# Decode attention with feed-forward on one core: q projection with column groups and held weights, q spread by one matmul per batch row and two quads, TensorE loop from unit 1

## Chip, core, metric

One core of one Trainium2 chip. The metric is the device time of one launch in microseconds (us). Most runs of the kernel before lie between 993.6 and 994.7 us; 4 of its 36 runs in this study are over 995 us.

## The reference

```python
# B=4 rows, one token each; D=640; 32 heads of 192; 4096 cached keys and values per head; F=1536
h   = x + attention(layernorm(x))       # q = ln(x) @ wq ; softmax(q k^T / sqrt(192)) v ; @ wo
out = h + (silu(ln(h) @ w_gate) * (ln(h) @ w_up)) @ w_down
```

The two caches are 403 of the 424 MB that the kernel reads. Every cached byte is used once.

## The kernel before

The work is cut in 32 *units*: a unit is four heads (one *quad*) of one batch row. For each unit one key load and one value load of 6.29 MB come in, all issued by SyncE on one DMA queue, in program order. I call them K0, K1, ... and V0, V1, ... by unit. There are two key buffers and one value buffer.

```python
def load_k(u):   # two slots: K(u) may start when the products of unit u-2 are done
    deps = [lambda: tk["tt", u - 2, NQ - 1]] if u >= 2 else ([wq_used] if u == 1 else [])
def load_v(u):   # one slot: V(u) may start when the values matmuls of unit u-1 are done
    deps = [(lambda: tk["pv", u - 1]) if u >= 1 else wq_used]

load_k(0); load_k(1)
for u in range(NU - 1):
    load_v(u)
    if u + 2 < NU:
        load_k(u + 2)
```

So the queue gets K0, K1, V0, K2, V1, K3, V2, ... and V1 is issued only after the values matmuls of unit 0, which run inside unit 1. One unit, shortened:

```python
for k in range(4):           # four quarters of the keys
    tt(u, k)                 # VectorE: keys * q, 128x6144, waits K(u) and q of this unit (qbc[u // 2])
    if k == 3: pv(u - 1)     # TensorE: values matmuls of the unit before -> frees the value slot
    red(u, k)                # TensorE: 12 identity matmuls fold 192 products to 16 (waits all of q)
    rsum(u, k - 1)           # VectorE
# then max, exp (ScalarE), and so on
```

The start, before unit 0: q projection (80 matmuls of 384 columns, four column groups), four copies of q, and the *spread*: each row's q is copied to the 32 partitions of its head by 128 small matmuls and 16 ScalarE evictions. The TensorE program is a hardware loop over units 2 to 31 (`pr.roll("pe", 2, NU)`); units 0 and 1 stand unrolled before it.

## Time and profile before

| | |
|---|---|
| time | 994.0 us (993.87 to 994.07), profiled span 992.2 us |
| busy | TensorE 58%, VectorE 56%, ScalarE 11% |
| DMA | 428 GB/s over the span; nine tenths or more in 39 of 40 slices |
| steady part | one key and one value load per 29.07 us, 433 GB/s |

From the page of the kernel before: busy time with share and number of instructions, the DMA row of the 40 slices (tenths busy), and the first two lines of the chain of work that ended last.

```profile
PE 577.5 (58%) x4656; PEld 117.2 (12%) x3248; DVE 552.7 (56%) x451; ACT 108.0 (11%) x348; POOL 3.4 (0%) x19
...
DMA  9999999999999999999999999999999999999997
...
DMA 67%; PE 18%; DVE 13%; SPq 1%; issue 0%; ACT 0%; DVEq 0%
DMA k<-in_A_k_cache_dram 60%; PE pb L152 11%; DVE prod L403 11%; DMA v<-in_A_v_cache_dram 8%; PE pb L455 5%; PE pb L411 2%; DVE sc L416 1%; SPq L350 0%; PE pb L551 0%; SPq L354 0%; PE pb L561 0%; PE pb L495 0%; DVE guT L557 0%; PE pb L480 0%; PE pb L298 0%
```

The kernel is bound by the DMA engines. The timeline of SyncE's queue in the kernel before (start us, duration, line, what is issued):

```profile
30.27 0.33 SPq L342 DMA_DIRECT2D k<-in_A_k_cache_dram  x1
30.64 0.43 SPq L350 DMA_DIRECT2D v<-in_A_v_cache_dram  x1
53.98 0.33 SPq L342 DMA_DIRECT2D k<-in_A_k_cache_dram  x1
76.36 0.33 SPq L350 DMA_DIRECT2D v<-in_A_v_cache_dram  x1
76.74 0.43 SPq L342 DMA_DIRECT2D k<-in_A_k_cache_dram  x1
101.11 0.33 SPq L350 DMA_DIRECT2D v<-in_A_v_cache_dram  x1
```

These are K1, V0, K2, V1, K3, V2. When V1 is issued at 76.36 us, only K2 is still moving. The first product starts when K0 has landed (VectorE, same timeline):

```profile
37.47 6.63 DVE L403 TENSOR_TENSOR prod<-k,qball 128x6144 f16<-128x6144 bf16 x2 [12.55 <-DMA k<-in_A_k_cache_dram]
```

And the windows view around V1's issue (window, length, then busy us and instructions of PE, PEld, DVE, ACT, POOL, the granted TensorE clock as a share of the full one, the DMA engines' share and GB/s; this view counts a packet whole in the window in which it starts, so a share can be over 1):

```profile
76.00:78.00 2.00, 2.00 (x17) 0.10 (x1) 0.42 (x1) 0.42 (x1) 0.00 (x0) 1.00 0.91 393
78.00:80.00 2.00, 1.83 (x19) 1.02 (x14) 0.91 (x2) 0.00 (x0) 0.00 (x0) 1.00 0.86 369
80.00:82.00 2.00, 0.76 (x4) 0.38 (x4) 1.49 (x5) 0.62 (x3) 0.00 (x0) 1.00 0.91 393
```

### The profile page before, as it was taken

Reading aid. Unit: us, or ns where it says so; the run is one execution under the profiler, and the core shown is the slowest. Engines: PE = TensorE matmul, PEld = TensorE weight load, DVE = VectorE, ACT = ScalarE, POOL = GpSimd, SP = SyncE. Lnnn points to the kernel's source line nnn. Section 1 sums busy time; section 2 is a strip of 40 time slices with the busy share of each in tenths; the row PEclk is TensorE's granted clock in tenths of the full one; section 3 lists DMA queues with packets and bytes.
Section 4 is the critical chain, followed back from the end, with each engine's and each line's share of the span. In section 5 each row is a group of like instructions: output and inputs, shape, how many; then the busy total and the mean of one; then the engine's idle time right before and its main releaser. Section 6 shows DMA issues by size and latency. Waiting matters only on the chain.

```text
span 992.2 us, 9305 instructions
## 1 busy us (share of the span) xinstructions
PE 577.5 (58%) x4656; PEld 117.2 (12%) x3248; DVE 552.7 (56%) x451; ACT 108.0 (11%) x348; POOL 3.4 (0%) x19
## 2 busy tenths in 40 slices
PE   0766555676555566655557655555665555666545
PEld 0101111111001111001111100111110011110032
DVE  1486645566654556664555666455666545566602
ACT  0311111110011110001111000111100111110011
POOL 1000000000000000000000000000000000000000
PEclk9788778887777888777788877788887778887775
DMA  9999999999999999999999999999999999999997
GB/s 402 427 436 433 423 438 438 420 442 436 420 444 434 422 444 430 426 440 430 430 440 428 432 440 424 432 442 422 436 440 422 438 438 422 440 436 420 421 417 306
DMA packets 12671, 424.48 MB, mean 428 GB/s; under 512 B 1264, under 2 KB 1264, under 8 KB 3952
## 3 DMA queue, kind: packets, MB, share of 16 engines
q1 hardware_dynamic: 12608, 424.29, 99.3%
q8 instruction: 7, 0.11, 0.0%
q14 instruction: 8, 0.07, 0.0%
q10 hardware_dynamic: 48, 0.01, 0.0%
HBM read 424.29 MB, written 0.01 MB: 428 GB/s over the span
## 4 chain that ended last, share of the span: by engine, by line
DMA 67%; PE 18%; DVE 13%; SPq 1%; issue 0%; ACT 0%; DVEq 0%
DMA k<-in_A_k_cache_dram 60%; PE pb L152 11%; DVE prod L403 11%; DMA v<-in_A_v_cache_dram 8%; PE pb L455 5%; PE pb L411 2%; DVE sc L416 1%; SPq L350 0%; PE pb L551 0%; SPq L354 0%; PE pb L561 0%; PE pb L495 0%; DVE guT L557 0%; PE pb L480 0%; PE pb L298 0%
## 5 line engine op out<-in xcount | busy, mean ns | idle before, releaser
L403 DVE TENSOR_TENSOR prod<-k,qball 128x6144 f16<-128x6144 bf16 x128 | 426.3, 3351 | 200.8 <-DMA k<-in_A_k_cache_dram 200.8
L152 PE MATMUL pb<-prod,identH 128*128 128x512 f16 x1408 | 385.8, 431 | 0.0
L411 PE MATMUL pb<-prod,identH 128*128 128x512 f16 x128 | 57.9, 452 | 340.5 <-DVE prod L403 334.2
L416 DVE TENSOR_REDUCE sc<-pb 128x32 f32<-128x512 f32 x128 | 88.0, 688 | 114.0 <-PE pb L152 114.0
L455 PE MATMUL pb<-v,pbuf 128*8 128x384 bf16 x2048 | 90.8, 330 | 9.2 <-DMA v<-in_A_v_cache_dram 9.1
L461 ACT ACTIVATE otmp<-pb,mask 128x192 f32<-128x192 f32 x32 | 13.4, 420 | 678.2 <-PE pb L455 678.2
L411 PEld LDWEIGHTS pb<-prod,identH 128*128 128x128 f16 x128 | 13.2, 103 | 588.0 <-DVE prod L403 466.7
L444 ACT ACTIVATE pbuf<-sc,negM 32x128 bf16<-32x128 f32 x128 | 73.4, 574 | 2.7 <-ACT negM L438 0.2
L455 PEld LDWEIGHTS pb<-v,pbuf 128*8 128x8 bf16 x2048 | 46.8, 87 | 121.3 <-DMA v<-in_A_v_cache_dram 86.6
L465 DVE SCALAR_TENSOR_TENSOR orow<-pb,mask,otmp 128x192 f32<-128x192 f32 x32 | 13.4, 418 | 77.4 <-ACT otmp L461 77.4
L444 ACT ACTIVATION_READ_ACCUMULATOR pbuf<-sc,negM 32x1 f32 x128 | 31.7, 248 | 0.0
L480 PE MATMUL pb<-pick,orow 128*64 128x2 f32 x384 | 22.3, 231 | 2.9 <-DVE orow L465 1.0
L438 ACT ACTIVATE negM<-pb 128x4 f32<-128x4 f32 x32 | 5.5, 173 | 161.1 <-PE pb L434 161.1
L470 PEld LDWEIGHTS pb<-lsb,halfm 128*128 128x128 f32 x64 | 12.1, 190 | 72.1 <-issue 71.1
L480 PEld LDWEIGHTS pb<-pick,orow 128*64 128x64 f32 x384 | 19.6, 174 | 6.2 <-DVE orow L465 1.7
L434 PE MATMUL pb<-negMc,ones_row 1*128 1x4 f32 x64 | 12.2, 258 | 11.9 <-DVE negMc L429 11.9
L429 DVE TENSOR_REDUCE negMc<-pb 1x4 f32<-1x128 f32 x32 | 8.9, 279 | 15.1 <-PE pb L425 15.1
L425 PE MATMUL pb<-identF,msb 128*1 128x128 f32 x64 | 12.2, 271 | 8.3 <-DVE msb L421 8.2
L298 PE MATMUL pb<-mv,quadm 128*128 128x2 f32 x4 | 1.2, 364 | 23.5 <-DVE mv L296 23.5
L434 PEld LDWEIGHTS pb<-negMc,ones_row 1*128 1x128 f32 x64 | 9.4, 183 | 21.3 <-DVE negMc L429 21.3
L294 DVE BATCH_NORM_STATS2 stats<-xrow 128x6 f32<-128x160 bf16 x1 | 0.3, 327 | 17.6 <-DMA xrow<-in_A_x_dram 17.6
L495 PE MATMUL pb<-wo_a,OTall 128*4 128x160 bf16 x144 | 5.2, 335 | 7.9 <-DMA wo_a<-in_A_wo_dram 6.7
(66 smaller groups left out, 92.0 us busy)
## 6 DMA issues: line engine op xcount, KB each, us to landing
k<-in_A_k_cache_dram SPq DMA_DIRECT2D x32, 6144.0 KB, 39.9
v<-in_A_v_cache_dram SPq DMA_DIRECT2D x31, 6144.0 KB, 25.7
wq_sb<-in_A_wq_dram SPq DMA_DIRECT2D x1, 7680.0 KB, 21.2
wo_a<-in_A_wo_dram SPq DMA_DIRECT2D x1, 5760.0 KB, 39.5
v<-in_A_v_cache_dram SPq DMA_DIRECT2D x1, 3072.0 KB, 20.6
wo_b<-in_A_wo_dram SPq DMA_DIRECT2D x1, 1920.0 KB, 13.7
wg_sb<-in_B_w_gate_dram SPq DMA_DIRECT2D x1, 1920.0 KB, 28.7
wu_sb<-in_B_w_up_dram SPq DMA_DIRECT2D x1, 1920.0 KB, 32.1
```

The costliest lines, as they stand in the source:

```text
L152: return e.add_instruction(mybir.InstMatmult(name=e.bass.get_next_instruction_name(), engine=mybir.EngineType.PE, start_tensor_calc=start, ...
L403: op("dve", lambda e: e.tensor_tensor(out=prod[BUF[k]][:, :, :], in0=kslot[u % 2][:, k * QT:(k + 1) * QT, :], in1=qball[:, u, None, :].bro ...
L411: op("pe", lambda e, j=j: (e.matmul if j == 0 else partial(held_matmul, e))(psR[k][:, 0:QT * R], lhsT=identH[:, :], rhs=prod[BUF[k]][:, :, ...
L416: op("dve", lambda e: e.tensor_reduce(sc[u % 2][:, k * QT:(k + 1) * QT], psR[k][:, 0:QT * R].rearrange("q (t r) -> q t r", r=R), AX.X, ALU ...
L425: op("pe", lambda e: e.matmul(psS[0:1, XT], lhsT=msb[:, 0:1], rhs=identF[:, :], start=True, stop=True), [g("rmax", u), g("negM", u - 1), p ...
L434: op("pe", lambda e: e.matmul(psS[:, XB], lhsT=ones_row[0:1, :], rhs=negMc[0:1, :], start=True, stop=True), [g("hmax", u), g("negM", u - 1 ...
L444: op("act", lambda e, h=h, r=r: e.activation(out=pbuf[r, :, h], in_=sc[u % 2][r, :], func=ACTF.Exp, bias=negM[r, h:h + 1], scale=alpha, ac ...
L455: op("pe", lambda e, t=t, n=n: e.matmul(psO[32 * n:32 * n + 8, 0:2 * DH], lhsT=pbuf[:, t:t + 2, :].rearrange("q t m -> q (t m)"), rhs=vslo ...
L461: op("act", lambda e: e.activation(out=otmp[:, :], in_=psO[:, 0:DH], func=ACTF.Copy, scale=mask[:, 0:1]), [g("pv", u), g("stt", u - 1), km ...
L465: op("dve", lambda e: e.scalar_tensor_tensor(out=orow[:, :], in0=psO[:, DH:2 * DH], scalar=mask[:, 1:2], in1=otmp[:, :], op0=ALU.mult, op1 ...
L470: op("pe", lambda e: e.matmul(psL[:, XL], lhsT=halfm[:, :], rhs=lsb[:, :], start=True, stop=True), [g("exp", u), g("otm", u - 1)], key=("l ...
L480: op("pe", lambda e, j=j, s=s, lo=lo: e.matmul(psL[64 * s:64 * s + 64, lo:lo + 2], lhsT=orow[:, j:DH:3], rhs=pick[:, s:4:2], start=True, s ...
```

## The change

Its intent is a shorter start and a smaller TensorE program: a head of the quad becomes a column group of the q projection, so that one weight load serves four matmuls; one 128x128 matmul spreads a row's q for two quads at once (16 matmuls for 128); and the loop starts one unit earlier.

```diff
+        for c in range(CD):                      # contraction chunk outermost
+            for k in range(4):
+                for n in range(4):
+                    rhs = ...                    # head n of two quads
+                    mm = partial(held_matmul, size=(128, 32), position=(0, 32 * n)) if k and HELD else ...
+                    a = op("pe", ... mm(e, PB[k][32 * n:32 * n + B, 0:2 * DH], lhsT=lnT[:, c, 0:B], rhs=rhs, ...))
+                if c == CD - 1:                  # the four copies now come together, at the end
+                    qcopy.append(op("act", ... qsb[:, k, :] <- PB[k] ...))
 ...
+        for i in range(NU // 2):
+            k, b, bank = i // B, i % B, psQ[i % 2]
+            a = op("pe", ... e.matmul(bank[:, 0:2 * DH], lhsT=sel[:, b, :], rhs=qsb[:, k, :], ...))
+            qbc[i] = op("act", ... qball[:, 8 * k + b:8 * k + b + B + 1:B, :] <- bank, scale=QS ...)
 ...
     def tt(u, k):
-            [landed["k", u], qbc[u // 2], last], key=("tt", u, k))
+            [landed["k", u], qbc[NU // 2 - 1 if FASTQ else u // 2], last], key=("tt", u, k))
 ...
-        pr.roll("pe", 2, NU)
+    pr.roll("pe", 1 if FASTQ else 2, NU)
```

Cut: the new layout of `OTall` (unit outermost), the larger `sel`, the code that computes loop waits, and two switches that stay off (`LOOPS`; `LATE`, which would load the last values before the last part of wo). A product now waits for the last of the 16 evictions of q, not for the one of its unit.

More of the change, by code (lines that the diff above doesn't have):

```diff
@@ L12 @@
 FP16 = mybir.dt.float16
-ROLL = True
+LOOPS = False
+FASTQ = True
+LATE = False
+HELD = True
 class Cfg:
@@ L46, in __init__ @@
         self.rolled = {}
+        self.shift = 0
     def op(self, eng, fn, deps=(), key=None):
@@ L112, in body @@
                     a, n, count = at[first], at[first + 1] - at[first], last - first
-                    delta = []
+                    plan = []
                     for j in range(n):
-                        w = [waits[a + s * n + j] for s in range(count)]
-                        d = [v - w[0][m][1] for m, (_, v) in enumerate(w[1])]
-                        for s in range(count):
-                            assert at[first + s] == a + s * n
-                            assert ops[a + s * n + j].needed == ops[a + j].needed
-                            assert [(k.name, v) for k, v in w[s]] == [
-                                (k.name, v + s * d[m]) for m, (k, v) in enumerate(w[0])], (j, s, w[0], w[s])
-                        delta.append(d)
+                        w = [{k.name: (k, v) for k, v in waits[a + s * n + j]} for s in range(count)]
+                        now = []
+                        for name in sorted(set().union(*w)):
+                            k, last = w[-1][name]
+                            d = last - w[-2][name][1]
+                            v = last - (count - 1) * d
+                            assert v > 0
+                            for s in range(count):
+                                assert at[first + s] == a + s * n
+                                assert ops[a + s * n + j].needed == ops[a + j].needed
+                                assert name not in w[s] and s < 2 or w[s][name][1] == v + s * d, (eng, j, s, name)
+                            now.append((k, v, d))
+                        plan.append(now)
                     for t, w in zip(ops[:a], waits[:a]):
@@ L127, in body @@
                     with self.nc.Fori(0, count, 1, engines=bass.OrderedEngineSet([e.engine]),
-                                      head_slot={e.engine: 0}) as s:
+                                      head_slot={e.engine: 0} if eng == "pe" else None) as s:
+                        self.shift = s
                         for j in range(n):
-                            for (k, v), d in zip(waits[a + j], delta[j]):
+                            for k, v, d in plan[j]:
                                 e.wait_ge(k, s * d + v)
                             one(e, ops[a + j])
+                        self.shift = 0
                     i = a + n * count
@@ L147, in emit, with held_matmul @@
         block.sync(run("sp"))
-def held_matmul(e, out, lhsT, rhs, start, stop):
+def held_matmul(e, out, lhsT, rhs, start, stop, size=(128, 128), position=(0, 0)):
     return e.add_instruction(mybir.InstMatmult(
         name=e.bass.get_next_instruction_name(), engine=mybir.EngineType.PE, start_tensor_calc=start,
-        stop_tensor_calc=stop, tile_size=(128, 128), tile_position=(0, 0), ldweights=False,
+        stop_tensor_calc=stop, tile_size=size, tile_position=position, ldweights=False,
         ins=[e.lower_ap(rhs), e.lower_ap(lhsT, for_matmul_weights=True)], outs=[e.lower_ap(out)]))
@@ L201, in build_kernel @@
     pbuf = sb("pbuf", [128, T, 4], BF16)
-    OTall = sb("OTall", [128, P, 3, B], BF16)
+    OTall = sb("OTall", [128, NU, 2, 3], BF16)
     qsb = sb("qsb", [128, 4, 2 * DH], BF16)
-    sel = sb("sel", [128, B, 32], BF16)
+    sel = sb("sel", [128, B, 128 if FASTQ else 32], BF16)
     identF = sb("identF", [128, 128], FP32)
@@ L282, in build_kernel @@
     op("dve", lambda e: e.memset(epsv[:, :], eps))
-    ksel = op("dve", lambda e: e.tensor_copy(
-        out=sel[:, :, :], in_=r32[:, 0:B][:, :, None].broadcast_to([128, B, 32])), [c1])
+    if FASTQ:
+        ksel = op("dve", lambda e: e.tensor_copy(
+            out=sel[:, :, :].rearrange("q b (h i) -> q b h i", h=4),
+            in_=identF[:, :].rearrange("q (h r) -> q r h", h=4)[:, 0:B, :, None].broadcast_to([128, B, 4, 32])), [c2])
+    else:
+        ksel = op("dve", lambda e: e.tensor_copy(
+            out=sel[:, :, :], in_=r32[:, 0:B][:, :, None].broadcast_to([128, B, 32])), [c1])
     kquad = op("dve", lambda e: e.tensor_scalar(
@@ L321, in build_kernel @@
     qcopy = []
-    for k in range(4):
+    if FASTQ:
         for c in range(CD):
-            for n in range(4):
-                p = 2 * (4 * (k // 2) + n) + k % 2
-                a = op("pe", lambda e, k=k, c=c, n=n, p=p: e.matmul(
-                    PB[k][32 * n:32 * n + B, 0:2 * DH], lhsT=lnT[:, c, 0:B],
-                    rhs=wqsb[:, c, p * 2 * DH:(p + 1) * 2 * DH], start=(c == 0), stop=(c == CD - 1)),
-                    [ln1, wq_land, zp])
-        qcopy.append(op("act", lambda e, k=k: e.activation(
-            out=qsb[:, k, :], in_=PB[k][:, 0:2 * DH], func=ACTF.Copy, scale=1.0), [a]))
+            for k in range(4):
+                for n in range(4):
+                    rhs = wqsb[:, c, 8 * k * DH:8 * (k + 1) * DH].rearrange("q (s d) -> q s d", s=2)[:, :, n * DH:(n + 1) * DH]
+                    mm = partial(held_matmul, size=(128, 32), position=(0, 32 * n)) if k and HELD else lambda e, *a, **kw: e.matmul(*a, **kw)
+                    a = op("pe", lambda e, k=k, c=c, n=n, rhs=rhs, mm=mm: mm(
+                        e, PB[k][32 * n:32 * n + B, 0:2 * DH], lhsT=lnT[:, c, 0:B], rhs=rhs,
+                        start=(c == 0), stop=(c == CD - 1)), [ln1, wq_land, zp])
+                if c == CD - 1:
+                    qcopy.append(op("act", lambda e, k=k: e.activation(
+                        out=qsb[:, k, :], in_=PB[k][:, 0:2 * DH], func=ACTF.Copy, scale=1.0), [a]))
+    else:
+        for k in range(4):
+            for c in range(CD):
+                for n in range(4):
+                    p = 2 * (4 * (k // 2) + n) + k % 2
+                    a = op("pe", lambda e, k=k, c=c, n=n, p=p: e.matmul(
+                        PB[k][32 * n:32 * n + B, 0:2 * DH], lhsT=lnT[:, c, 0:B],
+                        rhs=wqsb[:, c, p * 2 * DH:(p + 1) * 2 * DH], start=(c == 0), stop=(c == CD - 1)),
+                        [ln1, wq_land, zp])
+            qcopy.append(op("act", lambda e, k=k: e.activation(
+                out=qsb[:, k, :], in_=PB[k][:, 0:2 * DH], func=ACTF.Copy, scale=1.0), [a]))
     wq_used = a
@@ L362, in build_kernel, with load_wo @@
             load_k(u + 2)
-    wo_land = []
-    for lo, hi, t, deps in ((0, WA, woA, [lambda: tk["tt", NU - 2, NQ - 1]]), (WA, P, woB, [lambda: tk["red", NU - 1, NQ - 1]])):
-        a = dma("sp", lambda e, lo=lo, hi=hi, t=t: e.dma_start(
+    wo_land = {}
+    def load_wo(lo, hi, t, deps):
+        a = dma("sp", lambda e: e.dma_start(
             t[:, :, :, :].rearrange("q p j n -> q p (j n)"),
             wo[lo * 2 * DH:hi * 2 * DH, :].rearrange("(p q j) n -> q p (j n)", q=128, j=3)), sem(f"s_wo{lo}"), deps)
-        wo_land += [a] * (hi - lo)
-    load_v(NU - 1)
+        for p in range(lo, hi):
+            wo_land[p] = a
+    load_wo(0, WA, woA, [lambda: tk["tt", NU - 2, NQ - 1]])
+    if LATE:
+        load_v(NU - 1)
+    load_wo(WA, P, woB, [lambda: tk["red", NU - 1, NQ - 1]])
+    if not LATE:
+        load_v(NU - 1)
     k_free = [lambda: tk["tt", NU - 1, NQ - 1]]
@@ L383, in build_kernel @@
     qbc = {}
-    for i in range(NU // 2):
-        c = i * 2 // B
-        n, bank = c % 4, psQ[i % 2]
-        for s in range(2):
-            b = (2 * i + s) % B
-            for h in range(4):
-                k, lo = 2 * (c // 4) + h // 2, (h % 2) * DH
-                a = op("pe", lambda e, bank=bank, s=s, b=b, h=h, n=n, k=k, lo=lo: e.matmul(
-                    bank[32 * h:32 * h + 32, s * DH:(s + 1) * DH], lhsT=sel[32 * n:32 * n + B, b, :],
-                    rhs=qsb[32 * n:32 * n + B, k, lo:lo + DH], start=True, stop=True),
-                    [qcopy[k], qcopy[-1], ksel, qbc.get(i - 2)])
-        qbc[i] = op("act", lambda e, i=i, bank=bank: e.activation(
-            out=qball[:, 2 * i:2 * i + 2, :].rearrange("q u d -> q (u d)"), in_=bank[:, 0:2 * DH],
-            func=ACTF.Copy, scale=QS), [a])
+    if FASTQ:
+        for i in range(NU // 2):
+            k, b, bank = i // B, i % B, psQ[i % 2]
+            a = op("pe", lambda e, bank=bank, k=k, b=b: e.matmul(
+                bank[:, 0:2 * DH], lhsT=sel[:, b, :], rhs=qsb[:, k, :], start=True, stop=True),
+                [qcopy[k], qcopy[-1], ksel, qbc.get(i - 2)])
+            qbc[i] = op("act", lambda e, k=k, b=b, bank=bank: e.activation(
+                out=qball[:, 8 * k + b:8 * k + b + B + 1:B, :], in_=bank[:, 0:2 * DH].rearrange("q (s d) -> q s d", s=2),
+                func=ACTF.Copy, scale=QS), [a])
+    else:
+        for i in range(NU // 2):
+            c = i * 2 // B
+            n, bank = c % 4, psQ[i % 2]
+            for s in range(2):
+                b = (2 * i + s) % B
+                for h in range(4):
+                    k, lo = 2 * (c // 4) + h // 2, (h % 2) * DH
+                    a = op("pe", lambda e, bank=bank, s=s, b=b, h=h, n=n, k=k, lo=lo: e.matmul(
+                        bank[32 * h:32 * h + 32, s * DH:(s + 1) * DH], lhsT=sel[32 * n:32 * n + B, b, :],
+                        rhs=qsb[32 * n:32 * n + B, k, lo:lo + DH], start=True, stop=True),
+                        [qcopy[k], qcopy[-1], ksel, qbc.get(i - 2)])
+            qbc[i] = op("act", lambda e, i=i, bank=bank: e.activation(
+                out=qball[:, 2 * i:2 * i + 2, :].rearrange("q u d -> q (u d)"), in_=bank[:, 0:2 * DH],
+                func=ACTF.Copy, scale=QS), [a])
     BUF = (0, 1, 2, 0)
@@ L404, in tt @@
             out=prod[BUF[k]][:, :, :], in0=kslot[u % 2][:, k * QT:(k + 1) * QT, :],
-            in1=qball[:, u, None, :].broadcast_to([128, QT, DH]), op=ALU.mult),
-            [landed["k", u], qbc[u // 2], last], key=("tt", u, k))
+            in1=qball[:, bass.ds(u + 2 * pr.shift, 1), :].broadcast_to([128, QT, DH]), op=ALU.mult),
+            [landed["k", u], qbc[NU // 2 - 1 if FASTQ else u // 2], last], key=("tt", u, k))
     def red(u, k):
@@ L484, in otm @@
     def otm(u):
-        c, b = u // B, u % B
         op("dve", lambda e: e.tensor_tensor(
-            out=OTall[:, 2 * c:2 * c + 2, :, b], in0=psL[:, XO].rearrange("q (j a) -> q a j", a=2),
+            out=OTall[:, bass.ds(u + 2 * pr.shift, 1), :, :].rearrange("q u a j -> q (u a) j"), in0=psL[:, XO].rearrange("q (j a) -> q a j", a=2),
             in1=invL[:, :, None].broadcast_to([128, 2, 3]), op=ALU.mult),
@@ L495, in womm @@
                 a = op("pe", lambda e, j=j, n=n: e.matmul(
-                    psH[32 * n:32 * n + B, 0:DQ], lhsT=OTall[:, p, j, :],
+                    psH[32 * n:32 * n + B, 0:DQ], lhsT=OTall[:, p // 2 * B:p // 2 * B + B, p % 2, j],
                     rhs=w[:, p if p < WA else p - WA, j, n * DQ:(n + 1) * DQ], start=False,
@@ L502, in build_kernel @@
         pr.step("pe")
+        if u % 2 == 0:
+            pr.step("dve")
+            pr.step("act")
         for k in range(NQ):
@@ L525, in build_kernel @@
             otm(u - 1)
-    pr.step("pe")
-    if ROLL:
-        pr.roll("pe", 2, NU)
+    for eng in ("pe", "dve", "act"):
+        pr.step(eng)
+    pr.roll("pe", 1 if FASTQ else 2, NU)
+    if LOOPS:
+        pr.roll("dve", 1, NU // 2)
+        pr.roll("act", 1, NU // 2)
     u = NU - 1
     load_act = op("act", lambda e: e.activation(out=mv[:, 3:4], in_=epsv[:, 0:1], func=ACTF.Sqrt))
-    for p in range(P - 2):
+    early = WA if LATE else P - 2
+    for p in range(early):
         womm(p)
@@ L541, in build_kernel @@
     otm(u)
-    womm(P - 2)
-    wo_done = womm(P - 1)
+    for p in range(early, P):
+        wo_done = womm(p)
     zg = op("dve", lambda e: e.memset(PB[0][:, 0:FQ], 0.0), [g("red", u, NQ - 1), g("rsum", u, NQ - 1)])
```

## The prediction

> **What bounds the kernel now.** The DMA queue. The page's slices show the 16 DMA engines at nine tenths or more in 39 of 40 slices, 428 GB/s on average; TensorE is busy 58%, VectorE 56%. The chain of waits gives DMA 67% of the span. In the steady part every second key load on it lands 58.14 us after the last (226.72, then 284.86 us): 12.58 MB per 29.07 us, 433 GB/s. The Trainium skill ("DMA: Bandwidth & Descriptors", Bandwidth) puts the fabric ceiling at 435 GB/s; this trace agrees. The same 424.5 MB must move after the change, in the same order.
>
> **What the change touches, costed from the timeline.**
> - q projection: 80 matmuls take 24.97 to 30.22 us. The first twelve groups of four come 0.32 us apart, the rest about 0.16 us: the 384 moving columns set the pace, as the cold and warm clocks of the Trainium skill ("TensorE: Matmul & The Clock Gate", Part 1) would. Holding weights drops 60 of 80 loads, but they hide behind the matmuls: about 5 us again. The first value and second key load are released at about 30.2 us as now, while the first key load still moves (it lands at 37.4 us).
> - The four copies of q (0.49 us each) were staggered and ended at 30.77 us. With the contraction chunk outermost they come together at the end: about 31.7 us.
> - Spread of q: 128 matmuls become 16. But the 16 ScalarE evictions (0.463 us each, ten of them back to back, then 0.55) already set its pace, 31.2 to 39.1 us, and they stay. With one 128x128 matmul each on two banks I expect 0.46 to 0.55 us apiece, ending at 39.5 to 41 us.
> - The first product now waits for all of q: it starts at about 40 us instead of 37.47 us.
> - The TensorE loop from unit 1 and the new layout of OTall take nothing off a chain.
>
> **How much is on the critical path.** Almost nothing. A late first unit matters only if a load is issued after the queue ran dry. The tightest place: the second value load is issued at 76.36 us, and the load then in flight lands at about 81.3 us (an estimate: the fourth key load lands at 110.43 us, less two loads of 14.53 us). That is 4.9 us of slack; a delay of 2 to 3.5 us fits. At the end, the last value chunk lands at 975.26 us and a serial chain of 15 us follows. The change touches there only the stride at which four columns of OTall are loaded (24 matmuls, 1.0 us).
>
> **Predicted: 994.0 us, range 993.0 to 995.4 us.** Faster by over 2%: 0.01. Within 2%: 0.98. Slower by over 2%: 0.01.
>
> **What would show it right.** Matmuls fall by 112, weight loads by about 172. Copies of q end near 31.7 us, the last eviction of the spread near 40 us, the first product right after it. From the fourth key landing (110.4 us) on, landings agree within 0.3 us; DMA stays at nine tenths or more; the serial tail stays 15 us. PE busy falls by only a few us.
>
> **What would make it wrong.** If the spread ends past about 42 us, the second value load comes after the queue has emptied and each further us is lost. If held weights break the running of four column groups at once, the projection could take up to four times as long (20 us), past the first key landing, and cost 8 us or more. If the DMA stream itself ran differently, the steady 29.07 us per unit would move; nothing in the change suggests it.

## The result

| | before | after |
|---|---|---|
| median | 994.04 us (993.87 to 994.43, 4 runs) | 997.58 us (995.43 to 1000.25, 4 runs) |
| span of the profiled run | 992.2 us | 993.6 us |

The ratio is 1.0036, 95% interval 1.0012 to 1.0061: slower, by less than 2%, and outside the predicted range. A ratio here is the mean time of one kernel's runs over that of the other's of the same rounds, so it is not quite the ratio of the medians. Besides the mean, the spread grew from half a microsecond to five.

The page of the kernel after, the same parts:

```profile
PE 583.4 (59%) x4544; PEld 114.2 (11%) x3076; DVE 552.6 (56%) x451; ACT 108.1 (11%) x348; POOL 3.4 (0%) x19
...
DMA  9999999999999999999999999999999999999997
...
DMA 64%; PE 20%; DVE 13%; SPq 1%; issue 1%; ACT 0%; ACTq 0%
```

The counts fell as meant (112 matmuls, 172 weight loads), and the slices show nothing: a slice is 25 us long. Now the issues, the first products and the windows of the kernel after:

```profile
30.15 0.33 SPq L372 DMA_DIRECT2D k<-in_A_k_cache_dram  x1
30.52 0.44 SPq L380 DMA_DIRECT2D v<-in_A_v_cache_dram  x1
56.41 0.33 SPq L372 DMA_DIRECT2D k<-in_A_k_cache_dram  x1
79.15 0.33 SPq L380 DMA_DIRECT2D v<-in_A_v_cache_dram  x1
```

```profile
31.75 7.96 ACT L428 ACTIVATE qball<-pb 128x384 bf16<-128x384 f32 x16 [0.43 <-PE pb L425]
...
39.74 6.63 DVE L451 TENSOR_TENSOR prod<-k,qball 128x6144 f16<-128x6144 bf16 x2 [14.77 <-ACT qball L428]
```

```profile
76.00:78.00 2.00, 2.00 (x46) 1.02 (x48) 2.00 (x2) 0.00 (x0) 0.00 (x0) 1.00 0.91 393
78.00:80.00 2.00, 2.00 (x33) 0.54 (x21) 0.43 (x2) 0.42 (x1) 0.00 (x0) 1.00 0.12 49
80.00:82.00 2.00, 1.94 (x13) 0.41 (x4) 0.19 (x2) 0.00 (x0) 0.00 (x0) 1.00 1.30 393
```

VectorE was released not by the key load any more but by the last eviction of q (31.75 + 7.96 = 39.71 us). Everything behind it is 2.3 to 2.8 us later, V1 is issued at 79.15 us, and the DMA share of the window from 78 to 80 us is 0.12, against 0.86 before: the queue ran dry, though SyncE issued the load before the last packet of K2 had ended. The view overstates it, as it shows that hardly a packet *starts* there, and a packet of these loads (49,152 bytes) takes 1.82 us; by the packets in flight the engines were 57% busy in this window, against 97% before. By the packet records of the two traces, K3's last packet ends 73.7 us after K0's before and 75.1 us after: 1.3 us lost there, of the 1.4 us by which the spans differ. From then on loads follow every 14.53 us in both, and the serial end takes the same time (16.9 us from the first matmul on the last value chunk to the end before, 16.6 us after).

That explains the profiled run, which is the fastest of the four, and not those of 997 to 1000 us.

### The profile page after: what moved, and what is told of

Its sections match the earlier page's. It is cut to its first block, busy times and chain, and to the rows that moved or that the text cites. A ratio compares the mean times of both kernels' runs of the same rounds, so it can differ in the third digit from the quotient of the medians.

```text
span 993.6 us, 9031 instructions
## 1 busy us (share of the span) xinstructions
PE 583.4 (59%) x4544; PEld 114.2 (11%) x3076; DVE 552.6 (56%) x451; ACT 108.1 (11%) x348; POOL 3.4 (0%) x19
## 4 chain that ended last, share of the span: by engine, by line
DMA 64%; PE 20%; DVE 13%; SPq 1%; issue 1%; ACT 0%; ACTq 0%
DMA k<-in_A_k_cache_dram 56%; PE pb L164 12%; DVE prod L451 12%; PE pb L503 5%; DMA wd_sb<-in_B_w_down_dram 3%; DMA v<-in_A_v_cache_dram 3%; DMA xrow<-in_A_x_dram 2%; PE pb L459 2%; DVE sc L464 1%; PE pb L425 1%; SPq L380 0%; SPq L415 0%; SPq L384 0%; ACT qball L428 0%; ACT qsb L349 0%
## 5 line engine op out<-in xcount | busy, mean ns | idle before, releaser
L164 PE MATMUL pb<-prod,identH 128*128 128x512 f16 x1408 | 390.4, 434 | 0.0
L459 PE MATMUL pb<-prod,identH 128*128 128x512 f16 x128 | 59.7, 467 | 336.8 <-DVE prod L451 336.8
L492 ACT ACTIVATION_READ_ACCUMULATOR pbuf<-sc,negM 32x1 f32 x128 | 31.7, 248 | 0.0
L469 DVE TENSOR_REDUCE msb<-sc 128x1 f32<-128x128 f32 x32 | 9.2, 286 | 1.1
```

Of the source, the lines that this page charges most:

```text
L164: return e.add_instruction(mybir.InstMatmult(name=e.bass.get_next_instruction_name(), engine=mybir.EngineType.PE, start_tensor_calc=start, ...
L459: op("pe", lambda e, j=j: (e.matmul if j == 0 else partial(held_matmul, e))(psR[k][:, 0:QT * R], lhsT=identH[:, :], rhs=prod[BUF[k]][:, :, ...
L492: op("act", lambda e, h=h, r=r: e.activation(out=pbuf[r, :, h], in_=sc[u % 2][r, :], func=ACTF.Exp, bias=negM[r, h:h + 1], scale=alpha, ac ...
```

## The experiments

Theory A: the late q makes the first product late, V1 is issued after the queue has run dry, and each further microsecond is lost. Rivals: B, the TensorE loop from unit 1 delays unit 1; C, something at the end of the kernel, by the new layout of `OTall`. Below, *V1* is the issue time of the second value load in the trace of that run, and *idle* is worked out from the trace's packet records: at each moment between 60 and 130 us, 16 less the packets in flight, over 16, summed. It is the DMA time lost around V1, good to about 0.1 us (it depends on whether the few packets outside the load queue are counted).

### Undoing one part, and adding one part

`after_again` is the changed kernel unaltered.

> The changed kernel, unaltered. Theory A (the first product starts 2.3 us later because it waits for all of q, so the second value load is issued after the DMA queue has run dry, and each us beyond a slack of 1 to 2 us is lost): again slower than before by 1 to 6 us, with a spread of several us between runs, and in its trace a pause of the DMA engines between the third key load and the second value load about as long as the loss. Theory B (the TensorE loop from unit 1 delays unit 1): the same total, but the time from the start of unit 1's first product to the issue of the second value load is longer than the 17.9 us of before by more than 1 us. Theory C (the end of the kernel: the new layout of OTall): the loss appears after the last value chunk.

996.18 us median (995.07 to 997.31), ratio 1.0018 (1.0001 to 1.0034). Its trace is of a 997.12 us run: first product 39.35 us, V1 80.82 us, idle 3.0 us.

`own_unit`, own waits:

```diff
-            [landed["k", u], qbc[NU // 2 - 1 if FASTQ else u // 2], last], key=("tt", u, k))
+            [landed["k", u], qbc[u // 8 * 4 + u % 4 if FASTQ else u // 2], last], key=("tt", u, k))
```

> The changed kernel, but each product waits only for the q of its own unit, not for all of q. Theory A: the first product starts at 37.5 us again, the second value load is issued at 76.4 us, no pause of the DMA, and the time is that of before: ratio 1.000 within 0.001, spread under 1 us. Theories B and C: still slower by 1 to 6 us.

995.0 us (994.1 to 995.5), ratio 1.0011 (0.9994 to 1.0027). The traced run, 994.1 us, is as A says: first product 36.48 us, V1 73.56 us, no idle. But two of four runs are over 995.4 us. A alone doesn't account for those.

`loop_from_2`:

```diff
-    pr.roll("pe", 1 if FASTQ else 2, NU)
+    pr.roll("pe", 2, NU)
```

> The changed kernel with the TensorE loop from unit 2, as before. Theory A: as slow as the changed kernel (1 to 6 us over before, with a spread of several us), first product at about 39.7 us. Theory B: the time of before, 994.0 us.

995.06 us (994.55 to 996.22), ratio 1.0011 (0.9995 to 1.0028); first product 39.85 us, V1 79.24 us, idle 1.4 us. Undoing either part alone moved the median by about 1.1 us on the same chip, and neither brought back the time of before. The intervals overlap, so on times alone this is weak; the traces are what counts.

`before_all_q`, the wait for all of q put into the kernel before:

```diff
-            [landed["k", u], qbc[u // 2], last], key=("tt", u, k))
+            [landed["k", u], qbc[NU // 2 - 1], last], key=("tt", u, k))
```

> The kernel before, with the one wait added: each product waits for all of q. Theory A: the first product moves from 37.5 to about 39.2 us (+1.7 us), which about uses up the slack: 994 to 996 us, more spread than before, and a small pause or none of the DMA. Theories B and C: exactly the time of before, ratio 1.000.

994.97 us (994.63 to 995.23), ratio 1.0009 (0.9993 to 1.0026). First product 40.31 us, V1 77.94 us, idle 0.6 us. Without the end's new layout and without the loop from unit 1, the wait alone opens the gap in the trace: against C, for A. The interval includes 1 here too.

### Dose

One, or two, idle products of 3.35 us in front of the first real product of the kernel *before*:

```diff
+    late = None
+    for _ in range(1):      # 2 in before_delay2
+        late = op("dve", lambda e: e.tensor_tensor(
+            out=prod[2][:, :, :], in0=kslot[0][:, 0:QT, :],
+            in1=qball[:, 0, None, :].broadcast_to([128, QT, DH]), op=ALU.mult),
+            [landed["k", 0], qbc[0], late])
```

> The kernel before with one idle product of 3.35 us put in front of its first real product; nothing else of the change is in it. Theory A: the first product starts at about 40.9 us, the second value load is issued at 79 to 80 us, after the queue has run dry; 1 to 3 us lost (995 to 997 us) with a spread of a microsecond or more, as the changed kernel. Theories B and C: 994.1 us, as the delay would be hidden.

994.73 us (994.36 to 996.38), ratio 1.0008 (0.9991 to 1.0024): less than expected. V1 78.51 us, idle 0.8 us: it was issued half a microsecond sooner than the earliest time I had reckoned with (79 us).

> The kernel before with two idle products (6.7 us) in front of its first real product. Theory A: the slack of 1 to 2 us is gone and every further us is lost: about 5 us over before (998 to 1000 us), 3.35 us more than with one. Theories B and C: 994.1 us or at most 2 us more.

998.42 us (998.09 to 999.51), ratio 1.0038 (1.0021 to 1.0055). V1 83.48 us, idle 5.7 us. The windows view of `before_delay2`:

```profile
76.00:78.00 2.00, 0.63 (x4) 0.04 (x1) 2.00 (x2) 0.00 (x0) 0.00 (x0) 1.00 0.91 393
78.00:80.00 2.00, 2.00 (x10) 0.06 (x1) 2.00 (x2) 0.00 (x0) 0.00 (x0) 1.00 0.12 49
80.00:82.00 2.00, 2.00 (x40) 0.82 (x40) 2.00 (x2) 0.00 (x0) 0.00 (x0) 1.00 0.00 0
82.00:84.00 2.00, 2.00 (x39) 0.73 (x29) 0.43 (x2) 0.42 (x1) 0.00 (x0) 1.00 0.00 0
84.00:86.00 2.00, 2.00 (x12) 0.22 (x2) 0.36 (x1) 0.00 (x0) 0.00 (x0) 1.00 1.24 393
```

The queue runs dry at the same point, 78 to 80 us, as in the kernel after (by the packets in flight 56% busy there, 2% and nothing in the two windows behind it); it only stays dry longer. That is the clearest test of A: a delay in an otherwise untouched kernel costs time in exactly this place.

### A remedy that failed

With K3 issued ahead of V1, the queue should be fed 1.7 us sooner. (`own_swap` adds the own waits.)

```diff
+        if u == 1:
+            load_k(u + 2)
         load_v(u)
-        if u + 2 < NU:
+        if u + 2 < NU and u != 1:
             load_k(u + 2)
```

> The changed kernel with one pair of loads exchanged: the fourth key load is issued ahead of the second value load, so the queue is fed as soon as unit 1's last product is done, about 1.7 us before the values matmuls end. The late first product stays. Theory A: the loss shrinks by 1.5 to 1.7 us, so most of it goes in runs with the warm clock: about 994 to 996 us, first product still at about 39.7 us. Theories B and C: no change, 995 to 997 us.

1003.21 us (1001.12 to 1004.68), ratio 1.0080.

> The changed kernel with both remedies: a product waits for the q of its own unit alone, and the fourth key load goes ahead of the second value load. Theory A: over 5 us of slack, no pause of the DMA whatever the clock: 993.9 to 994.4 us, spread under 0.7 us as before. If the 994.1 to 995.5 us of the kernel with own waits alone has another cause than the supply of the queue, that spread stays.

1002.13 us (1001.73 to 1002.49), ratio 1.0078. In `own_swap` the gap at 78 us did go (0.94 busy from 78 to 82 us), but a longer one came 30 us later. SyncE's timeline (a row may merge two issues) and three windows of `own_swap`:

```profile
53.21 21.38 SPq L372 DMA_DIRECT2D k<-in_A_k_cache_dram  x2
75.94 39.14 SPq L380 DMA_DIRECT2D v<-in_A_v_cache_dram  x2
115.12 0.43 SPq L372 DMA_DIRECT2D k<-in_A_k_cache_dram  x1
```

```profile
106.00:110.00 4.00, 0.02 (x4) 0.02 (x6) 0.00 (x0) 0.00 (x0) 0.00 (x0) 0.50 0.34 147
110.00:114.00 4.00, 4.00 (x52) 1.78 (x56) 0.00 (x0) 0.00 (x0) 0.00 (x0) 0.50 0.00 0
114.00:118.00 4.00, 3.94 (x40) 1.09 (x22) 0.98 (x2) 0.42 (x1) 0.00 (x0) 1.00 0.64 197
```

V1 now lands after K3. V2 waits for the values matmuls on V1, and K4, whose buffer was long free, stands behind V2 in SyncE's program and is issued only at 115.12 us. I had reasoned about each load's own wait and forgotten that one sequencer issues them in order. The times of the two runs say nothing against A or B; the new gap hides what they were to show.

### The second cause

The own waits once more, for another trace:

> The kernel with own waits once more, for its spread and a second trace. Theory A: 994.0 to 995.5 us as before; the loss of a slower run comes from a later issue of the second value load (cold TensorE in units 0 and 1), so a trace of a slow run shows that load issued after 77 us, a trace of a fast one before it. If the trace is of a run over 995 us and that load is issued before 77 us, another cause is at work.

995.45 us (993.89 to 996.17), ratio 1.0005 (0.9991 to 1.0019). Now the traced run is the longest of the five, 996.17 us (the long trace below). Its first product starts at 36.40 us, as early as in the trace of 994.1 us, and yet V1 is issued at 80.12 us. TensorE's timeline of unit 1 in the long trace, `own_unit_again`; the last line is the first matmul of the loop:

```profile
56.96 0.38 PE L473 MATMUL pb<-identF,msb 128*1 128x128 f32 x2 [1.10 <-DVE msb L469]
57.71 0.38 PE L482 MATMUL pb<-negMc,ones_row 1*128 1x4 f32 x2 [0.37 <-DVE negMc L477]
65.25 0.61 PE L459 MATMUL pb<-prod,identH 128*128 128x512 f16 x1 [7.17 <-issue]
```

and the same matmul in the kernel after (the run of 995.43 us):

```profile
64.33 0.61 PE L459 MATMUL pb<-prod,identH 128*128 128x512 f16 x1 [2.89 <-DVE prod L451]
```

In the long trace unit 1's first product had ended at 60.9 us; TensorE starts 4.3 us later, and the idle time is put to "issue", which means that the profile knows no wait for it. In the trace of the kernel after, 0.06 us pass. What comes just before is an instruction fetch: the DMA packets of 16,384 bytes on the queue of kind "instruction". In all ten traces that have a late loop start, this packet starts 0.1 to 2.5 us after the product has ended, and TensorE begins 2.5 to 2.7 us after the packet starts (three of the ten put the wait down to the product, though it had ended 3.3 to 4.0 us before):

| trace | loop start | first product of that unit ends | fetch packet starts | TensorE starts | late by |
|---|---|---|---|---|---|
| `after_again` | unit 1 | 63.0 | 64.4 | 66.98 | 4.0 |
| `own_unit_again` | unit 1 | 60.9 | 62.7 | 65.25 | 4.3 |
| `own_k0split` | unit 1 | 60.4 | 61.1 | 63.71 | 3.3 |
| `own_k0split_late` | unit 1 | 59.1 | 61.1 | 63.80 | 4.7 |
| `all_q_sooner` | unit 1 | 60.6 | 60.8 | 63.4 | 2.8 |
| `swap_k3_v1` | unit 1 | 63.9 | 66.4 | 69.00 | 5.1 |
| before | unit 2 | 84.4 | 84.9 | 87.47 | 3.1 |
| `before_all_q` | unit 2 | 85.9 | 87.4 | 89.91 | 4.0 |
| `before_delay1` | unit 2 | 86.5 | 86.8 | 89.31 | 2.8 |
| `before_delay2` | unit 2 | 91.5 | 91.6 | 94.11 | 2.6 |
| `after` | unit 1 | 64.3 | 57.2 | 64.33 | 0.1 |
| `own_unit` | unit 1 | 59.6 | 51.8 | 59.69 | 0.1 |
| `own_swap` | unit 1 | 61.1 | 57.2 | 61.12 | 0.1 |

Of the nine traces with the new q code and the loop from unit 1, the six with the fetch after 60 us are late and the three with the fetch before 58 us are not. The three traces of the new q code with the loop from unit 2 have no late start, in unit 1 or 2. The records do not name the engine that a fetch is for; but where only TensorE's loop is moved to unit 2, the second fetch moves from between 60 and 71 us to 84 and 87 us (`own_loop2`, `loop_from_2`).

The kernel before has the same late start, but in unit 2, and so have its three variants. Its line (TensorE's timeline of the kernel before):

```profile
87.47 0.60 PE L411 MATMUL pb<-prod,identH 128*128 128x512 f16 x1 [6.22 <-issue]
```

There it costs nothing: V2 is issued at 101.11 us, while K3 is still moving (its products start, on landing, at 110.45 us). The change moved the entry into the loop, with its fetch, from unit 2 into unit 1, which has next to no slack.

The Trainium skill, "Runtime: NRT & Kernel Launch", Instruction fetch mechanics, says that instructions come in blocks of 16 KiB by DMA, and that a taken branch to a block which isn't there forces a fetch before execution can go on. The traces agree in the block size and in the stall; that the way into the loop takes such a branch, no run shows.

### Testing the remedies

`own_k0split`: own waits, and K0 in four quarters with a semaphore each.

```diff
+        if u == 0:
+            s = src(kc, u).rearrange("q (t d) -> q t d", d=DH)
+            for k in range(NQ):
+                landed["k0", k] = dma("sp", lambda e, k=k: e.dma_start(
+                    kslot[0][:, k * QT:(k + 1) * QT, :], s[:, k * QT:(k + 1) * QT, :]), sem(f"s_k0_{k}"), deps)
+            return
 ...
-            [landed["k", u], ...
+            [landed["k0", k] if u == 0 else landed["k", u], ...
```

> Own waits, and the first key load in four quarters, so the first product starts when q is there (about 32 us) and not when all of the first key load has landed (36.5 us). Theory A: the second value load is issued at 69 to 72 us, over 5 us ahead of the 77 us at which the queue runs dry; 993.7 to 994.3 us with a spread under 0.7 us. If the spread of 1.4 us of own waits alone comes from elsewhere, it stays.

994.48 us (994.06 to 994.62), ratio 1.0001 (0.9988 to 1.0015). The spread is small, but the step I expected did not happen: the first product starts at 31.82 us, and V1 is still issued at 78.41 us. The identity matmuls of unit 0 wait for all of q anyway (their bank is one of the spread's), so the third product starts only at 45.28 us, and TensorE is 3.3 us late at the loop. Idle 0.4 us.

`all_q_sooner` keeps the wait for all of q, but shares the evictions between ScalarE and VectorE on four banks:

```diff
-    psQ = [PB[7], PB[3]]
+    psQ = [PB[7], PB[3], PB[0], PB[1]]
 ...
+            if i % 2 == 0:
+                qbc[i] = op("act", ... e.activation(out=dst, in_=got, func=ACTF.Copy, scale=QS), [a])
+            else:
+                qbc[i] = op("dve", ... e.tensor_scalar(out=dst, in0=got, scalar1=QS, ..., op0=ALU.mult), [a])
```

> The changed kernel with its wait for all of q kept, but the 16 evictions shared by ScalarE and VectorE over four banks, so that all of q is there at about 36 us. Theory A: only the time matters, not what is waited for: first product at about 36.5 us, the time of the kernel with own waits (994.0 to 995.5 us). If waiting for all of q costs by itself, 995 to 997 us.

994.73 us (994.08 to 995.42), ratio 1.0003 (0.9988 to 1.0018): first product 36.86 us, and times like those of own waits. What a product waits for doesn't matter; when it comes does. V1 77.87 us, because TensorE is late at the loop here too.

`own_k0split_late` was to be a faster version: it also sets the change's own switch `LATE`.

> The kernel with own waits and the quartered first key load, and the last value load put ahead of the second part of wo in the DMA queue (the change's own switch LATE). The last value chunk should land about 4.5 us earlier (1.97 MB at 433 GB/s), its serial chain of 15 us then ends before the last weights have landed or just after: 990.5 to 992.5 us, which would beat both kernels.

994.77 us (994.27 to 995.68), ratio 1.0005 (0.9992 to 1.0019). The matmuls on the last value chunk did come earlier (971.62 us, against 977.00 us in the kernel after), but the gain is given back: TensorE's timeline of `own_k0split_late` shows the feed-forward's second weights arriving late.

```profile
981.61 1.77 PE L611 MATMUL pb<-wg_sb,lnT 128*4 128x384 bf16 x20 [1.90 <-DVE lnT L325]
...
985.67 1.77 PE L611 MATMUL pb<-wu_sb,lnT 128*4 128x384 bf16 x20 [2.29 <-DMA wu_sb<-in_B_w_up_dram]
```

In this trace the end waits for the bytes left to move, so the order of these two loads gained nothing.

### Both causes taken away

`own_loop2` has both edits, own waits and the loop from unit 2.

> The changed kernel with own waits and with the TensorE loop from unit 2. If the loop start at unit 1 is the second cause: 993.7 to 994.4 us with the spread of before, TensorE starts unit 1 within 0.1 us of its first product's end, the second value load is issued before 76.5 us. If the loop is innocent: 994 to 996 us, as own waits alone.

993.90 us (993.69 to 994.49, 5 runs); before in the same rounds 994.28 us (993.83 to 995.82); ratio 0.9995 (0.9981 to 1.0009). V1 74.20 us, no idle, TensorE 0.06 us after its product. From its timelines:

```profile
60.23 0.61 PE L459 MATMUL pb<-prod,identH 128*128 128x512 f16 x1 [2.89 <-DVE prod L451]
...
74.20 0.33 SPq L380 DMA_DIRECT2D v<-in_A_v_cache_dram  x1
```

`oldq_loop1` sets `FASTQ = False` (the old q code and its waits) and rolls from unit 1.

> The old q code (switch FASTQ off) with the new layout of OTall and the TensorE loop from unit 1: the loop alone. If the loop start at unit 1 is the second cause: some runs 1 to 3 us over before, and in a trace of such a run an instruction fetch and a late start of TensorE of 3 to 5 us in unit 1; median 994.5 to 996 us. If innocent: 994.1 us as before.

994.04 us (993.62 to 994.32), ratio 0.9996 (0.9982 to 1.0010). V1 74.95 us, no idle, no late start: a miss of my expectation. So the loop from unit 1 is not a cost by itself. This program has three fetch packets in the first 70 us (35.2, 44.3, 62.7 us) where the changed kernel has two, as its start is longer. That the stall depends on where the loop falls in the fetched blocks fits this, but no run shows it. The run also clears the new layout of `OTall`, which it has.

`own_loop2_k0split` is `own_loop2` with K0 in quarters.

> Both causes gone and the first key load in quarters, so the second value load is issued at about 70 us, some 7 us before the queue runs dry. If supply of the queue in the first two units is all there is: 993.7 to 994.3 us, spread under 0.5 us, at least as good as before, whose runs now and then reach 995 us. If something else is in the change, 994.5 us or more.

994.31 us (993.85 to 994.53), ratio 0.9997 (0.9983 to 1.0010); V1 74.09 us and not 70, for the reason seen in `own_k0split`; no idle.

### All traces but the two of exchanged loads, in one table

| run | first product | TensorE late in unit 1 | V1 issued | idle |
|---|---|---|---|---|
| own_unit | 36.48 | 0.1 | 73.56 | 0.0 |
| own_loop2_k0split | 32.82 | 0.1 | 74.09 | 0.0 |
| own_loop2 | 36.76 | 0.1 | 74.20 | 0.0 |
| oldq_loop1 | 37.42 | 0.1 | 74.95 | 0.0 |
| before | 37.47 | 0.1 | 76.36 | 0.2 |
| all_q_sooner | 36.86 | 2.8 | 77.87 | 0.4 |
| before_all_q | 40.31 | 0.1 | 77.94 | 0.6 |
| own_k0split | 31.82 | 3.3 | 78.41 | 0.4 |
| before_delay1 | 40.93 | 0.1 | 78.51 | 0.8 |
| own_k0split_late | 32.06 | 4.7 | 78.66 | 0.8 |
| after | 39.74 | 0.1 | 79.15 | 1.1 |
| loop_from_2 | 39.85 | 0.1 | 79.24 | 1.4 |
| own_unit_again | 36.40 | 4.3 | 80.12 | 2.1 |
| after_again | 39.35 | 4.0 | 80.82 | 3.0 |
| before_delay2 | 44.03 | 0.1 | 83.48 | 5.7 |

Whatever made V1 late, the idle time follows its issue. From 80.82 to 83.48 us (+2.66) the idle time grows by 2.64 us: slope one. Drawn back from there, the line meets zero at 77.8 us (83.48 - 5.65). The kernel before issues at 76.36 us, 1.4 us ahead of that. The profiled span goes with the idle time: over that of before it grows by the idle time added, to within 0.7 us, in all but `all_q_sooner` (1.1 us more, which nothing here explains).

The table hides one thing that varies from execution to execution. Nine of these traces have K0 whole and no late start in unit 1. In five of them (`own_unit`, `own_loop2`, `oldq_loop1`, `before_all_q`, `before_delay1`) the mean granted clock between the first product and V1 was 0.87, and V1 came 37.1 to 37.6 us after the first product; in four (before, `after`, `loop_from_2`, `before_delay2`) it was 0.79 to 0.81, and V1 came 38.9 to 39.5 us after it. (In the trace of before, 11 identity matmuls took 4.74 us where the granted clock was 0.50 and 2.54 us where it was 1.00.) So about 1.9 us of V1's time go with the clock and not with the edit: of the 5.6 us by which V1 is sooner in `own_unit` than in `after`, 3.3 us are the first product's, and of the 6.6 us between the two traces of own waits 4.3 us are the late start. Why the clock differed, no run shows.

## Why the prediction was wrong

- **Right:** what bounds the kernel; the counts (minus 112 and 172); the projection at about 5 us (25.03 to 30.12 us); the copies' end (31.3 us, predicted 31.7); the spread paced by its 16 evictions and ending near 40 us (39.71 us); the first product at about 40 us (39.74 us); the end of the kernel. The Trainium skill's page on the clock gate ("TensorE: Matmul & The Clock Gate", Part 1) has a clock of half or full speed; in the windows shown here the granted clock is 0.50 or 1.00, which agrees.
- **Failed, a term of the sum: "That is 4.9 us of slack".** The runs show about 1.4 us. I had taken the landing of the load in flight as the moment at which the queue runs dry. (1) From issue to the first packet of V1 on an empty queue 0.96 us pass (79.15 to 80.11 us in the kernel after; 0.96 us in `before_delay2`, too). (2) The 16 engines do not finish together: in the kernel after they end K2 between 78.6 and 80.4 us, at 79.2 us in the mean. (3) My landing time of 81.3 us was itself 0.9 us after K2's last packet (80.4 us in the trace of before). That is 3.1 of the 3.5 us missing. The delay of 2.8 us was inside the predicted 2 to 3.5 us; it just did not fit. The prediction had named this very loss, for a spread that "ends past about 42 us"; the spread ended at 39.71 us, and the loss was there.
- **Failed, a step: "The TensorE loop from unit 1 and the new layout of OTall take nothing off a chain."** True of `OTall`. The entry into the loop, though, brought an instruction fetch into unit 1 which held TensorE for 3 to 5 us in six of the nine traces with the new q code and the loop from unit 1. The trace of before has the same stall in unit 2, where it is free; the prediction does not mention it.
- **Missed: the spread.** The kernel before is mostly steady, as its supply just holds. With no slack left, what varies from run to run in units 0 and 1 goes straight into the time: the fetch (3 to 5 us), and about 1.9 us that go with the granted clock.
- **"DMA stays at nine tenths or more"** held in the slices and was the wrong test: a gap of 1 to 2 us doesn't show in a slice of 25 us. The sharper test of the prediction, landings within 0.3 us from K3 on, failed: K3 landed at 111.54 us, in the kernel before at 110.42 us.

What is settled: the delay of V1, put into the kernel before, costs time in the place that A names; each of the two parts alone makes V1 late in some traces of the new q code, and with both taken away the time of before is back (0.9995). On times alone the single parts are not settled: their intervals include 1. What stays open: why the fetch comes in time in some executions of one and the same program (51.8 us) and not in others (62.7 us); why the loop from unit 1 with the old q code had no stall; and what made the slowest run, 1000.25 us, of which no trace is left: `after_again` had both causes at once, lost 3.0 us and took 997.12 us. No version beats the kernel before: 993.90 us is within its noise. The new q code did not bring q sooner (last eviction 39.71 us, before 39.14 us), and a first product at 32.82 us gained nothing either (`own_loop2_k0split`).

## What to carry to other kernels

In a kernel bound by DMA, ask for each early load how long before its issue the queue would run dry, and count that from issue to first packet and for the engine that finishes first, not from issue to landing. Look at it in windows of 2 us, and mind that a packet counts there in the window in which it starts. And treat the entry into a hardware loop as an event with a cost: put it where there is slack.

## What the Trainium skill lacked or had wrong

- "Runtime: NRT & Kernel Launch", Instruction fetch mechanics, calls the crossing of a block "mostly hidden" and warns of a stall at a taken branch, without a duration. With the DMA engines saturated, ten traces show TensorE starting 2.6 to 5.1 us late behind a fetch, 2.5 to 2.7 us after the fetch's first packet had started; which of the two cases it is, they do not show.
- No page tells what a fetch costs the data: a packet of 16,384 bytes took 0.88 to 1.11 us here. In the five traces with a fetch at 35.2 to 35.5 us K0 lands at 37.2 to 37.6 us, in the nine others with K0 whole at 36.2 to 36.7 us.
- "DMA: Bandwidth & Descriptors", Latency and other measured facts, gives about 0.6 us to the first byte for a load issued as here, and does not say from when. From the start of the issue to the first packet the traces show 0.96 to 0.97 us, from the end of the issue instruction (0.33 us) 0.63 to 0.64 us, so only the second way of counting agrees.
- No page gives a figure for how far apart the engines finish a load: K2's 128 packets ended on the first engine at 78.6 us, on the mean one at 79.2 us and on the last at 80.4 us (kernel after).
